# A gated attention and MLP decode step: small loads behind a first activation, and a last weight transfer in three pieces

## The chip, the cores and the metric

The kernel runs on one core of one Trainium2 chip. The metric is the device time of one execution in microseconds (us); lower is better. Three runs of the kernel before gave 137.19, 137.25 and 137.4 us, so the median is 137.25 us.

## What is computed

One token passes through two branches that a scalar gate mixes. The reference, cut to what matters:

```python
# x: 1 x 1 x 576 (A_x serves both branches); 32 query heads, 16 key/value heads, head size 128
W = 4096                                        # only the last 4096 positions of the cache are used
q = x @ wq                                      # 576 -> 32*128
k, v = k_cache[:, :, Sk-W:], v_cache[:, :, Sk-W:]   # 16 heads x 4096 x 128, bf16 each
a = softmax(q k^T * 128**-0.5) v @ wo           # 4096 -> 576
b = gelu(x @ w1 + b1) @ w2 + b2                 # 576 -> 4608 -> 576, tanh form of gelu
g = sigmoid((x * gate_w).sum())
out = g * a + (1 - g) * b
```

Nearly all of the bytes are read once: 16 heads of K and of V at 1 MB each, and four weight matrices of some 5 MB each, 53.6 MB in all. The arithmetic is small beside it.

## The kernel before

**Loads.** All big loads go out on SyncE's queue (SP). They come in this order: K of head 0 (line 89), two quarters of wq (line 106), K of head 1, the other two quarters of wq, then K and V tiles by turns with five pieces of w1 among them, then wo in four transfers (line 426), and at last w2 in four tiles `w2_t` of nine "rows" each (line 436; a row is 576 columns for each of 128 partitions). The first three w2 tiles come in one transfer each. The last one is cut in two by `cut = (0, 6, RJ)` on line 434: rows 0 to 5, then rows 6 to 8. The four small loads go out on ScalarE's queue (ACT): `x9` and `gw9` (line 117, x and the gate weights, 18 bytes for each of 128 partitions), `b1g` (line 118) and `b2_row` (line 119). They are the first instructions of ACT. The trace calls these loads x, gw, b1g and b_row, and w1 and w2 both w_t.

**What holds a load back.** K and V tiles share ten buffers, weights eight. Beyond that each load takes one of eight semaphores in turn, so that a ninth load is issued only when the one that had its semaphore has landed. In the trace of before, the first eight loads are the four small ones and K0, wq 0, wq 1 and K1. The third quarter of wq waits for x, the fourth for K0, K2 for gw, the first piece of w1 for b1g, K3 for b_row. All engines issue in the order in which the code is written (`manual_schedule`).

**Compute.** K tiles are transposed on TensorE (PE) against an identity matrix (line 189), four 128x128 blocks into one PSUM tile `tp`, of which there are three. VectorE (DVE, line 198) and ACT (line 200) copy these tiles to SBUF by turns. The scores (line 215), a softmax for each four heads (from line 233 on) and the values (line 275) follow, with lags of one to five heads. x is doubled into `x2` by four DVE instructions (line 179) that stand ahead of the first copy of line 198 in DVE's order. The gate is computed on lines 289 to 301, between the transposes of K0 and the product with wq (line 312). ACT's first instruction that needs a function table is the copy on line 200; `ident`, the identity, is built by GpSimd (POOL) from line 131 on.

**The end.** `row_matmul` (line 476) multiplies one row of wo or w2 in four matmuls of 144 columns, one for each quarter of the output. For w2, all rows of a tile follow each other, so the last tile takes 24 matmuls on rows 0 to 5 and 12 on rows 6 to 8. After the last one DVE forms `y` (line 506), and SP stores it (line 509).

Of the kernel before, what the change touches and what calls it, by code (L numbers as in the profile page):

```python
# [8 lines left out]
FP32 = mybir.dt.float32  # L9
BF16 = mybir.dt.bfloat16  # L10
ACT = mybir.ActivationFunctionType
# [5 lines left out]
def kernel(  # L17
# [15 lines left out]
    nc = tc.nc  # L33
# [11 lines left out]
    RJ = 9  # L45
    NG = F // (P * RJ)
# [22 lines left out]
    small = ctx.enter_context(tc.tile_pool(name="small", bufs=2))  # L69
# [42 lines left out]
    gw9 = const.tile([P, NM], BF16, name="gw9")  # L112
    b1g = const.tile([NG, F // NG], BF16, name="b1g")
    b2_row = const.tile([1, D], BF16, name="b2_row")
    for dst, src in ((x9, A_x.rearrange("a b d -> (a b d)")), (gw9, gate_w)):
        v = src.rearrange("(i o m) -> i o m", o=1, m=NM).to_broadcast([P // 2, 2, NM])
        nc.scalar.dma_start(out=dst[:], in_=v)
# [25 lines left out]
    for o in range(2):  # L143
        nc.vector.tensor_reduce(
            out=par[:, o : o + 1],
            in_=ident_f[:].rearrange("p (i o) -> p o i", o=2)[:, o, :],
# [7 lines left out]
        out=turn[:].rearrange("p j (h q) -> p j h q", h=OJ),  # L154
        in_=ident[:].rearrange("p (o q j) -> p j o q", o=1, j=OJ).to_broadcast(
            [P, OJ, OJ, P // OJ]
        ),
# [4 lines left out]
        out=m_r[:], in_=ident_f[:].rearrange("p (s r) -> p r s", r=R), axis=AX.X, op=ALU.add  # L162
# [3 lines left out]
        out=m_hl[:], in_=ident_f[:].rearrange("p (h q) -> p h q", h=OJ), axis=AX.X, op=ALU.add  # L166
# [117 lines left out]
    for i in range(NBL):  # L284
# [5 lines left out]
        out=junk9[:], in0=x9[:], in1=gw9[:], scale=1.0, scalar=0.0,  # L290
# [11 lines left out]
        out=omg[:], in0=g_t[:], scalar1=-1.0, scalar2=1.0, op0=ALU.mult, op1=ALU.add  # L302
# [20 lines left out]
    for g in (1, 3):  # L323
        for hl in range(HB):
            lo = R * g + 2 * hl
            nc.vector.tensor_copy(  # L326
                out=qz[:, hl::HB, lo : lo + 2],
                in_=q_ps[:].rearrange("p o (b r) -> p (o b) r", r=R)[:, :, 2 * hl : 2 * hl + 2],
# [95 lines left out]
    for i in range(NOG // 2):  # L424
        t = w_pool.tile([P, WMAX], BF16, name="wo_t", tag="w")
        nc.sync.dma_start(
            out=t[:, 0 : 2 * OJ * D].rearrange("p (o n) -> p o n", o=2),
            in_=wo_view[:, 2 * i : 2 * i + 2, :],
# [2 lines left out]
    w2_t = []  # L431
    for g in range(NG):
        t = w_pool.tile([P, WMAX], BF16, name="w2_t", tag="w")
        cut = (0, RJ) if g < NG - 1 else (0, 6, RJ)
        for lo, hi in zip(cut, cut[1:]):
            nc.sync.dma_start(out=t[:, lo * D : hi * D], in_=w2_view[g, :, lo * D : hi * D])
        w2_t.append(t)
# [4 lines left out]
        out=sg[:],  # L442
# [14 lines left out]
    for j in range(OJ):  # L457
# [3 lines left out]
        out=ow_m[:],  # L461
# [6 lines left out]
        out=ow_f[:].rearrange("p j o -> p (j o)"), in_=ow_m[:], axis=AX.X, op=ALU.add  # L468
# [17 lines left out]
    for o in range(NOG):  # L486
# [8 lines left out]
        out=a_sb[:], in0=a_ps[:], scalar1=g_t[:, 0:1], scalar2=None, op0=ALU.mult  # L495
# [5 lines left out]
    for g in range(NG):  # L501
# [5 lines left out]
        out=y[:], in0=b_ps[:], scalar=omg[:, 0:1], in1=a_sb[:], op0=ALU.mult, op1=ALU.add  # L507
    )
    nc.sync.dma_start(
        out=out.rearrange("a b (t n) -> (a b t) n", t=NQ), in_=y[0 : 32 * (NQ - 1) + 1 : 32, :]  # L510
# [31 lines left out]
```

## Time and profile before

| | |
|---|---|
| median of 3 runs | 137.25 us |
| the profiled execution | 137.34 us |
| its span (first to last instruction) | 135.5 us |
| mean granted TensorE clock | 0.779 |
| PE busy | 101.2 us, 75% |
| DVE busy | 57.4 us, 42% |
| ACT busy | 42.0 us, 31% |
| POOL busy | 1.4 us, 1% |
| moved by DMA | 53.88 MB, mean 398 GB/s over the span |
| chain that ended last | DMA 89%, PE 6% of the span |

The profiled execution takes 1.84 us more than its span; this rest lies outside the instructions. An engine's share of the span tells how long it worked, not whether anyone waited for it. The chain that ended last follows the waits back from the last instruction and is the better guide here. Of the DMA queues, q1 is SP's, q10 is ACT's, and q8 and q14 carry instructions ("instruction" in the page's third part). A DMA share of 1.00 means that all 16 DMA engines were busy.

### The profile page before, as it was taken

How to read it: one execution, taken by the hardware profiler on the slowest of the kernel's cores; microseconds unless marked ns; L12 is line 12 of the kernel's file. 1: busy time of each engine (PE TensorE's matmuls, PEld its weight loads, DVE VectorE, ACT ScalarE, POOL GpSimd, SP SyncE). 2: the span in 40 equal slices, each digit the busy share in tenths (PEclk: the TensorE clock that was granted, in tenths of full speed). 3: DMA queues.
4: the chain of work that ended last, by engine and by line, in shares of the span. 5: the costliest groups of instructions: out<-in, count | busy, mean ns of one | idle time of the engine just before them, and what ended most of it. 6: DMA issues, size and time to landing. Idle time of an engine off the chain costs nothing.

```text
span 135.5 us, 3928 instructions
## 1 busy us (share of the span) xinstructions
PE 101.2 (75%) x1779; PEld 81.8 (60%) x1779; DVE 57.4 (42%) x127; ACT 42.0 (31%) x75; POOL 1.4 (1%) x7
## 2 busy tenths in 40 slices
PE   0386857989969997979999986999695946343361
PEld 0376844668747876867868964788475844233350
DVE  5271521663468375735566357375732140010001
ACT  0360330454356165524356251554322000000000
POOL 4000000000000000000000000000000000000000
PEclk9999996589689999996589996589687555555555
DMA  4999999999999999999999999999999999999930
GB/s 116 412 428 419 418 432 430 424 421 428 426 423 428 430 412 426 423 431 419 432 424 423 426 415 429 426 418 426 428 423 426 420 416 424 424 434 419 401 126 3
DMA packets 8035, 53.88 MB, mean 398 GB/s; under 512 B 1101, under 2 KB 1102, under 8 KB 2514
## 3 DMA queue, kind: packets, MB, share of 16 engines
q1 hardware_dynamic: 7720, 53.61, 94.5%
q8 instruction: 14, 0.23, 0.6%
q10 hardware_dynamic: 298, 0.02, 0.1%
q14 instruction: 3, 0.02, 0.0%
HBM read 53.62 MB, written 0.00 MB: 396 GB/s over the span
## 4 chain that ended last, share of the span: by engine, by line
DMA 89%; PE 6%; DVE 1%; SPq 1%; issue 0%; DVEq 0%
DMA k_t<-in_A_k_cache_dram 30%; DMA w_t<-in_B_w_dram 15%; DMA wo_t<-in_A_wo_dram 15%; DMA v_t<-in_A_v_cache_dram 15%; DMA wq_t<-in_A_wq_dram 11%; DMA x<-in_A_x_dram 4%; PE tp L189 3%; PE s_ps L215 1%; PE o_ps L275 1%; DVE kT L198 1%; DVE mx L233 0%; PE b_ps L476 0%; PE mb L248 0%; SPq L96 0%; PE pT L260 0%
## 5 line engine op out<-in xcount | busy, mean ns | idle before, releaser
L189 PE MATMUL tp<-ident,k_t 128*128 128x128 bf16 x512 | 52.1, 252 | 10.6 <-DMA k_t<-in_A_k_cache_dram 8.6
L198 DVE CAST kT<-tp 128x512 bf16<-128x512 f32 x64 | 43.5, 690 | 33.8 <-PE tp L189 32.1
L200 ACT CAST kT<-tp 128x512 bf16<-128x512 f32 x64 | 37.5, 586 | 53.7 <-PE tp L189 53.3
L189 PEld LDWEIGHTS <-k_t 128*128 128x128 bf16 x512 | 37.4, 112 | 15.5 <-DMA k_t<-in_A_k_cache_dram 10.0
L275 PEld LDWEIGHTS <-v_t 128*128 128x128 bf16 x512 | 22.8, 103 | 6.6 <-issue 6.4
L275 PE MATMUL o_ps<-et,v_t 128*128 128x2 bf16 x512 | 26.3, 166 | 0.3 <-DVE et L264 0.3
L215 PE MATMUL s_ps<-kT,qz 128*32 128x512 bf16 x128 | 15.0, 465 | 0.7 <-DVE qz L326 0.7
L359 PE MATMUL h_ps<-x,w_t 128*128 128x2 bf16 x162 | 10.4, 199 | 0.0
L359 PEld LDWEIGHTS <-w_t 128*128 128x128 bf16 x162 | 10.1, 158 | 0.0
L476 PE MATMUL b_ps<-w_t,gt 128*1 128x144 bf16 x144 | 5.2, 319 | 5.7 <-DMA w_t<-in_B_w_dram 5.7
L476 PE MATMUL a_ps<-wo_t,ow 128*1 128x144 bf16 x128 | 4.5, 319 | 5.7 <-DMA wo_t<-in_A_wo_dram 4.5
L476 PEld LDWEIGHTS <-gt 128*1 128x1 bf16 x144 | 4.1, 115 | 6.7 <-issue 6.5
L476 PEld LDWEIGHTS <-ow 128*1 128x1 bf16 x128 | 3.6, 116 | 6.3 <-issue 5.2
L215 PEld LDWEIGHTS <-qz 128*32 128x32 bf16 x128 | 3.3, 95 | 4.5 <-issue 2.3
L312 PE MATMUL q_ps<-x,wq_t 128*128 128x2 bf16 x144 | 4.4, 166 | 2.0 <-DMA wq_t<-in_A_wq_dram 1.9
L312 PEld LDWEIGHTS <-wq_t 128*128 128x128 bf16 x144 | 4.2, 102 | 2.4 <-DMA wq_t<-in_A_wq_dram 2.4
L506 DVE SCALAR_TENSOR_TENSOR y<-b_ps,omg,a_sb 128x144 bf16<-128x144 f32 x1 | 0.4, 368 | 11.2 <-PE b_ps L476 11.2
L494 DVE TENSOR_SCALAR a_sb<-a_ps,g_t 128x144 f32<-128x144 f32 x1 | 0.4, 368 | 9.1 <-PE a_ps L476 9.1
L252 ACT ACTIVATE pr<-s_ps,nb 128x512 bf16<-128x512 f32 x4 | 2.7, 687 | 3.5 <-DVE nb L249 3.2
L237 PE MATMUL mT<-ident_f,mx 128*1 128x128 f32 x4 | 1.2, 295 | 3.4 <-DVE mx L233 3.4
L233 DVE TENSOR_REDUCE mx<-s_ps 128x1 f32<-128x512 f32 x4 | 2.7, 684 | 1.3 <-PE s_ps L215 1.3
L260 PE MATMUL pT<-ident,pr 128*128 128x128 bf16 x16 | 2.3, 289 | 0.7 <-ACT pr L252 0.7
(59 smaller groups left out, 26.3 us busy)
## 6 DMA issues: line engine op xcount, KB each, us to landing
k_t<-in_A_k_cache_dram SPq DMA_DIRECT2D x16, 1024.0 KB, 19.8
v_t<-in_A_v_cache_dram SPq DMA_DIRECT2D x16, 1024.0 KB, 19.7
wq_t<-in_A_wq_dram SPq DMA_DIRECT2D x4, 1152.0 KB, 12.1
w_t<-in_B_w_dram SPq DMA_DIRECT2D x4, 1152.0 KB, 20.5
wo_t<-in_A_wo_dram SPq DMA_DIRECT2D x4, 1152.0 KB, 21.0
w_t<-in_B_w_dram SPq DMA_DIRECT2D x3, 1296.0 KB, 21.4
w_t<-in_B_w_dram SPq DMA_DIRECT2D x1, 864.0 KB
w_t<-in_B_w_dram SPq DMA_DIRECT2D x1, 576.0 KB
```

The costliest lines, as they stand in the source:

```text
L189: nc.tensor.matmul(tp[:, c * P : (c + 1) * P], lhsT=k_tiles[h][:, i * BC + c, :], rhs=ident[:], start=True, stop=True,)
L198: nc.vector.tensor_copy(out=dst, in_=tp[:])
L200: nc.scalar.copy(out=dst, in_=tp[:])
L215: nc.tensor.matmul(s_tiles[b][32 * t : 32 * (t + 1), :], lhsT=qz[:, h, lo : lo + 32], rhs=kT[h][:, i * BC * P : (i + 1) * BC * P], start=( ...
L233: nc.vector.tensor_reduce(out=mx[:], in_=s_ps[:], axis=AX.X, op=ALU.max)
L237: nc.tensor.transpose(out=mT[:], in_=mx[:], identity=ident_f[:])
L252: nc.scalar.activation(out=pr[:], in_=s_ps[:], func=ACT.Exp, bias=nb[:, 0:1], scale=SCALE, accum_out=sums[:, b : b + 1],)
L260: nc.tensor.transpose(out=pT[:, c, :], in_=pr[:, c * P : (c + 1) * P], identity=ident[:])
L275: nc.tensor.matmul(o_ps[:, 2 * h : 2 * h + 2], lhsT=v_tiles[h][:, i * BC + c, :], rhs=ets[b][:, c, col : col + 2], start=(i == 0 and c == ...
L312: nc.tensor.matmul(q_ps[:, :, c], lhsT=wq_t[b // QP][:, off : off + Dh], rhs=x2[:, m, :], start=(b == 0), stop=(m == NM - 1), skip_group_c ...
L359: nc.tensor.matmul(h_ps[:, j, gl::GH], lhsT=t[:, off : off + U - RJ + 1 : RJ], rhs=x2[:, m, :], start=False, stop=(m == NM - 1), skip_grou ...
L476: nc.tensor.matmul(acc[32 * t : 32 * t + 1, :], lhsT=col, rhs=rows[:, t * DQ : (t + 1) * DQ], start=start, stop=stop,)
```

## The change

There are two edits.

1. Ahead of the small loads a one-element tile `warm` is set to zero by POOL and passed through `Exp` by ACT, in place. ACT issues in order, so its four small loads come behind this activation. The table load, which stood ahead of the first copy of line 200, comes ahead of the activation now. `warm` is read by nothing else.
2. The last w2 tile comes in three transfers, not two: rows 0 to 5, rows 6 and 7, and row 8. The matmuls and their order stay as they are.

```diff
     b2_row = const.tile([1, D], BF16, name="b2_row")
+
+
+    warm = small.tile([1, 1], FP32, name="warm", tag="warm")
+    nc.gpsimd.memset(warm[:], 0.0)
+    nc.scalar.activation(out=warm[:], in_=warm[:], func=ACT.Exp)
     for dst, src in ((x9, A_x.rearrange("a b d -> (a b d)")), (gw9, gate_w)):
         v = src.rearrange("(i o m) -> i o m", o=1, m=NM).to_broadcast([P // 2, 2, NM])
         nc.scalar.dma_start(out=dst[:], in_=v)
@@
         t = w_pool.tile([P, WMAX], BF16, name="w2_t", tag="w")
-        cut = (0, RJ) if g < NG - 1 else (0, 6, RJ)
+        cut = (0, RJ) if g < NG - 1 else (0, 6, 8, RJ)
         for lo, hi in zip(cut, cut[1:]):
             nc.sync.dma_start(out=t[:, lo * D : hi * D], in_=w2_view[g, :, lo * D : hi * D])
```

## The prediction

> **What bounds the kernel now.** I read the page's 40 slices first, then the chain that ended last, then the timeline of the last microseconds, and last the DMA share in short windows at both ends. All times are microseconds from the span's start.
>
> The page's DMA rows:
>
> ```profile
> DMA  4999999999999999999999999999999999999930
> GB/s 116 412 428 419 418 432 430 424 421 428 426 423 428 430 412 426 423 431 419 432 424 423 426 415 429 426 418 426 428 423 426 420 416 424 424 434 419 401 126 3
> ```
>
> From the second slice to the 38th the DMA engines are full. No engine's work counts there unless it empties SP's queue. What can move the time is the first slice, the last two, and the number of bytes or packets, and the change touches only these.
>
> The end, from the chain (start, length, what) and the timeline (start, length, engine, line, operation):
>
> ```profile
> 110.96 20.92 DMA w_t<-in_B_w_dram
> 131.88 0.04 issue
> 131.93 0.56 PE b_ps L476 x12
> ```
>
> ```profile
> 121.32 0.28 PE L476 MATMUL b_ps<-b_row,one_b 1*1 1x144 bf16 x4 [0.68 <-DVE b_ps L499]
> ...
> 130.88 0.89 PE L476 MATMUL b_ps<-w_t,gt 128*1 128x144 bf16 x24 [0.80 <-DMA w_t<-in_B_w_dram]
> ...
> 131.93 0.53 PE L476 MATMUL b_ps<-w_t,gt 128*1 128x144 bf16 x12 [0.16 <-DMA w_t<-in_B_w_dram]
> ...
> 132.51 0.37 DVE L506 SCALAR_TENSOR_TENSOR y<-b_ps,omg,a_sb 128x144 bf16<-128x144 f32 x1 [11.24 <-PE b_ps L476]
> 132.90 0.65 SPq L509 DMA_DIRECT2D out_dram<-y  x1
> ```
>
> The last three rows of w2 land at 131.88. Twelve matmuls (0.53), y and the store follow one after the other. Only the twelve matmuls can shrink here.
>
> The stream does not end at one moment. Windows of the end (stretch, length, busy time of PE, PEld, DVE, ACT, POOL, clock, DMA share, GB/s):
>
> ```profile
> 126.00:128.00 2.00, 0.96 (x34) 0.76 (x25) 0.00 (x0) 0.00 (x0) 0.00 (x0) 0.50 1.00 418
> 128.00:129.00 1.00, 0.17 (x8) 0.17 (x11) 0.00 (x0) 0.00 (x0) 0.00 (x0) 0.50 0.71 294
> 129.00:130.00 1.00, 1.00 (x36) 0.87 (x29) 0.00 (x0) 0.00 (x0) 0.00 (x0) 0.50 0.47 194
> 130.00:131.00 1.00, 0.20 (x12) 0.12 (x11) 0.00 (x0) 0.00 (x0) 0.00 (x0) 0.50 0.28 114
> 131.00:132.00 1.00, 0.84 (x28) 0.63 (x24) 0.00 (x0) 0.00 (x0) 0.00 (x0) 0.50 0.07 28
> ```
>
> A share of 0.28 is 4.5 of 16 engines. Some have finished by 129, and about five carry the end alone. A transfer lands with its slowest engine, so these few set the time. What made them late must be what not all engines carry alike. The page's instruction queue q8 is the candidate: 14 packets, 0.6% of 16 x 135.5, that is 13.0 in all and 0.93 for each, on one engine each.
>
> **Edit 2, the last tile in three transfers.** It removes nothing and adds one transfer. A piece has 128 partitions, so 8 packets for each of 16 engines, plus one that signals (q10's 298 packets are 261 rows of the four small loads and 37 more). So each engine gets 9 more packets. Their fixed price comes from the small loads, between 3 and 6:
>
> ```profile
> q10 hardware_dynamic: 168, 0.00, 3.1%
> ```
>
> 3.1% of 16 x 3 is 1.49, divided by 168: 9 ns, most of them 18 bytes. Nine of them are 0.08. The last landing goes from 131.88 to 131.96. Bounds: 0, and 0.25 if short packets cost three times as much.
>
> Behind it PE has 4 matmuls instead of 12. Four took 0.28 (b_row's row), 12 took 0.53, 24 took 0.89, so 8 more are about 0.25. Rows 6 and 7 land before row 8 by its 9 packets. Row 8 is a third of 432 KB, which took 131.88 - 130.84 = 1.04 in all (130.84 is the start at 130.88 less the same 0.04 of issue), so 0.35, and with its packets' price about 0.4. So their 8 matmuls (0.41 on that line) run from 131.6 to 132.0, just as row 8 comes. Then 131.96 + 0.05 + 0.28 = 132.29, against 132.46 now: **0.17 gained**. Bounds: 0.25 (free packets) and nothing (0.25 for packets). SP issues the extra load at about 113.7, when the second wo load returns its semaphore, 18 ahead of its landing. The store now waits for the third wo load's semaphore, back at 116.7 and long free at 132.5.
>
> The Trainium skill speaks against this edit: "DMA: Bandwidth & Descriptors", section Bandwidth (Measured), calls transfers under 64 KB descriptor-dominated and asks for 1 MiB or more, and its section on the anatomy of one DMA fits about 2.0 us fixed for each (on another issue path). The trace has a 432 KB transfer that lands 1.04 after the one ahead, about 425 GB/s, so that fixed part was hidden by the queue; by the page's fit unhidden, the sum would be near 139.
>
> **Edit 1, the loads behind an activation.** ACT's and SP's first rows:
>
> ```profile
> 0.73 0.62 ACTq L117 DMA_DIRECT2D x<-in_A_x_dram  x1
> 0.73 0.39 SPq L89 DMA_DIRECT2D k_t<-in_A_k_cache_dram  x1
> 1.19 0.90 SPq L106 DMA_DIRECT2D wq_t<-in_A_wq_dram  x2
> ...
> 2.13 0.78 SPq L89 DMA_DIRECT2D k_t<-in_A_k_cache_dram  x1
> ...
> 3.29 1.28 ACT L200 ACT_TABLE_LOAD   x1 [3.29 <-issue]
> ```
>
> *Moved on ACT.* The table load (1.28) goes to 0.73. The activation costs some 0.17 (ge, 128x1, line 296). So x is issued at about 2.2, 1.47 later, and gw, b1g and b_row as much. The four end at 4.8. The first copy on ACT starts at 6.62, so the table load was hidden and still is: **0**.
>
> *Who waits for x.* SP's third wq load waits for x's semaphore (2.8 by SP's waits) and goes out at 5.70; K2 (8.80) waits for gw, w1's first piece for b1g, K3 for b_row. Meanwhile K0, wq 0, wq 1 and K1 fill the queue until 13.91, when K1 lands. First packets come 1.03 after an issue (0.73 to about 1.76), so the third wq load may go out as late as 12.8: cover of 7.1 against 1.47. x landed 0.18 after K0, and gw 0.32 after wq 0 (8.47), so they may have waited for their turn behind these rather than for their issue. x lands between 5.7 and 7.2. Should the later place hand x a semaphore that follows SP's own loads, wq 2 waits for K0 (5.50) instead, the same.
>
> *Compute behind x.* DVE's four x2 instructions (5.78 to 6.41) stand ahead of its copies, so K0's transposes, the gate and the first wq products may come up to 1.5 later. PE then idles 1.30 until K1 lands and 1.69 until wq 3 (20.52): the lag is gone there. **0**. Without that cover it would be 1.5 on PE, but still not on the DMA stream, which PE reaches only through buffers.
>
> *POOL.* One memset more (0.1 by its rows) ahead of ident. DVE waits 2.53 for x behind that: **0**.
>
> *The stream's start.* Here is what may be won:
>
> ```profile
> 1.75:2.40 0.65, 0.00 (x0) 0.00 (x0) 0.62 (x7) 0.00 (x0) 0.23 (x1) 1.00 0.77 101
> 2.40:2.70 0.30, 0.00 (x0) 0.00 (x0) 0.30 (x3) 0.00 (x0) 0.00 (x0) 1.00 0.95 273
> 3.00:4.00 1.00, 0.00 (x0) 0.00 (x0) 0.25 (x2) 0.71 (x1) 0.00 (x0) 1.00 0.95 401
> ```
>
> In the first window 101 GB/s x 0.65 is 66 KB: eight packets of 8 KB. Half of the engines seem to start 0.65 late, and x's issue, 0.62 long, runs beside K0's. SP's first issues take 0.39, 0.45 (each of two) and 0.78, later ones 0.33. The bounds are 0 and 0.65 (where a late engine is also a last one). But the early eight packets were busy 0.77 x 16 x 0.65 = 8.0, 1.0 each, against 0.31 at full rate (8 KB at 428/16). So the early half had won almost nothing by 2.8, and the late half would win as little. I take 0.06 for K0's shorter issue (0.39 to 0.33) and 0.07 for the late half: **0.13 gained**.
>
> **Sum.** 0.17 + 0.13 = 0.30. The profiled execution goes from 137.34 (span 135.5, 1.84 around it) to 137.04 (span 135.2); the median, 0.09 below that execution, from 137.25 to **136.95**. A measurement of this kernel can tell some 0.2% (0.27) from no change; the forecast lies just beyond it.
>
> **Rivals.**
> - *Tail only.* The start has the same halves whether ACT issues or not, since the first packets' 1.0 sets it, and the packets of row 8 may eat more. 137.08 to 137.25. For it: those 1.0. Against it: the long SP issues. Chance 0.20.
> - *The late half comes in time.* All 16 engines start together and the last engines are of the late half: 0.35 (8 of 16 engines x 0.7) to 0.65 more than the tail alone, so 136.45 to 136.75. Against it: the 1.0 again. Chance 0.10.
> - *Slower: an instruction packet gets ahead of row 8.* One q8 packet starts at 132.04 now, just behind the stream; the window from 132 to 133 has its 16 KB. PE's progress seems to call it. With rows 6 and 7 started 0.3 earlier, it comes near 131.7. If it falls on one of the about five engines still streaming, before 131.96, row 8 lands some 0.93 later: 136.95 + 0.93 = 137.9. Five of 16 engines, less for timing: chance 0.12.
> - *The queue runs dry at the start.* It decides once x lands after about 12.8, as when ACT's loads wait for semaphores of big ones; each us beyond is one lost. Chance 0.06, 137.6 or more.
>
> **Chances.** The forecast has 0.52, about two thirds of it beyond 0.2%. Faster: 0.35 + 0.10 + 0.01 = 0.46. Same: 0.17 + 0.19 = 0.36. Slower: 0.18. The range 136.6 to 137.5 leaves out nearly all of the slower cases and the best start-up ones, 0.2 together.
>
> **What would show it.** ACT's table load stands at 0.73 and x's issue near 2.2. SP's first four issues shorten toward 0.33. If the start-up term is right, the first window has more than eight packets and K0 lands 0.1 before 5.50. If the covers hold, wq 3 is still what PE waits for near 20.4, and no DMA slice between is under 9. At the end, PE has a group of 8 and one of 4 matmuls, and y comes within 0.38 of the last landing (0.63 now). A last landing later than 131.96, or a third wq issue after 12.8, makes the prediction wrong.

## The result

The changed kernel takes 137.06 us (median of 22 runs, 136.7 to 137.53) against 137.36 us for the kernel before beside it (22 runs, 136.96 to 137.65). The ratio is 0.9981, with a 95% interval from 0.9973 to 0.9989: 0.26 us faster by the ratio (the two medians lie 0.30 apart), at the bound of 0.2% that was named. A second measurement gave 0.9987 (0.9973 to 1.0001). The forecast was 136.95 us, or 0.30 us faster.

**The profile after.** The DMA rows of the page have the same picture as before, a first slice not filled, then full, then two slices of end:

```profile
DMA  4999999999999999999999999999999999999930
GB/s 111 407 415 427 422 419 433 420 426 429 426 419 426 430 413 431 419 431 423 426 428 424 424 419 422 426 424 429 424 422 427 418 413 430 431 428 413 417 154 8
```

The first slice has not gained (111 GB/s, before 116). The timeline of the first microseconds shows why (start, length, engine, line, operation):

```profile
0.73 1.28 ACT L119 ACT_TABLE_LOAD   x1 [0.73 <-PEq L531]
0.73 0.09 POOL L118 MEMSET warm<- 1x1 f32 x1 [0.29 <-POOLq L531]
0.73 0.39 SPq L89 DMA_DIRECT2D k_t<-in_A_k_cache_dram  x1
...
0.86 0.64 ACTq L122 DMA_DIRECT2D x<-in_A_x_dram  x1
...
1.19 1.05 SPq L106 DMA_DIRECT2D wq_t<-in_A_wq_dram  x2
...
2.02 0.20 ACT L119 ACTIVATE warm<-warm 1x1 f32<-1x1 f32 x1
...
2.28 0.71 SPq L89 DMA_DIRECT2D k_t<-in_A_k_cache_dram  x1
...
5.66 1.46 PE L194 MATMUL tp<-ident,k_t 128*128 128x128 bf16 x12 [5.66 <-DMA k_t<-in_A_k_cache_dram]
```

x is issued at 0.86, while the table load is still running and 1.16 ahead of the activation. Here ACT's queue did not hold a DMA back for the engine's work in front of it. (The 0.13 fits the end of POOL's memset at 0.82, on which the activation itself waits; no run tests this.) So the small loads are behind the activation in the code only. They moved by 0.13 us (0.73 to 0.86) and not by 1.47, and SP's first four issues did not become shorter: 2.15 us in all (0.39, 1.05 and 0.71), before 2.07. K0 is there for PE at 5.66, 0.11 later than before:

```profile
5.55 3.88 PE L189 MATMUL tp<-ident,k_t 128*128 128x128 bf16 x32 [5.55 <-DMA k_t<-in_A_k_cache_dram]
```

The end, from the chain that ended last and from the timeline:

```profile
108.13 22.76 DMA w_t<-in_B_w_dram
130.89 0.04 issue
130.93 1.38 PE b_ps L481 x36
```

```profile
130.93 1.35 PE L481 MATMUL b_ps<-w_t,gt 128*1 128x144 bf16 x36 [0.81 <-DMA w_t<-in_B_w_dram]
...
132.34 0.37 DVE L511 SCALAR_TENSOR_TENSOR y<-b_ps,omg,a_sb 128x144 bf16<-128x144 f32 x1 [11.02 <-PE b_ps L481]
132.74 0.66 SPq L514 DMA_DIRECT2D out_dram<-y  x1
```

The chain is a different one now. Before, it ran from the landing of the last transfer at 131.88 to 12 matmuls. Now it runs from the landing of rows 0 to 5 at 130.89 to 36 matmuls without a gap: PE starts at 130.93 and is done at 132.31. By the trace's records of the semaphores, rows 6 and 7 landed at 131.64 and row 8 at 131.96, and PE did not wait for either. The wait of 0.16 ahead of the last twelve matmuls is gone, and so is the second start: 0.89 + 0.53 were 1.42, the 36 in one go are 1.35. y starts at 132.34, where the prediction had worked out 132.29 for the end of the matmuls, and 0.17 earlier than in the profile of before.

The last microseconds' windows (stretch, length, five engines' busy time, clock, DMA share, GB/s) show that the stream itself ends as before, with about five DMA engines of 16 (0.29 x 16 = 4.6) that carry it past 130:

```profile
129.00:130.00 1.00, 1.00 (x36) 0.91 (x29) 0.00 (x0) 0.00 (x0) 0.00 (x0) 0.50 0.53 212
130.00:131.00 1.00, 0.19 (x8) 0.07 (x7) 0.00 (x0) 0.00 (x0) 0.00 (x0) 0.50 0.29 115
131.00:132.00 1.00, 1.00 (x33) 0.81 (x32) 0.00 (x0) 0.00 (x0) 0.00 (x0) 0.50 0.12 44
```

### The profile page after: what moved, and what is told of

Read it like the earlier page. It is cut to its first block, busy times and chain, and to the rows that moved or that the text cites. A ratio compares the mean times of both kernels' runs of the same rounds, so it can differ in the third digit from the quotient of the medians.

```text
span 135.2 us, 3931 instructions
## 1 busy us (share of the span) xinstructions
PE 100.2 (74%) x1779; PEld 81.1 (60%) x1779; DVE 57.3 (42%) x127; ACT 42.1 (31%) x76; POOL 1.4 (1%) x8
## 3 DMA queue, kind: packets, MB, share of 16 engines
q1 hardware_dynamic: 7864, 53.61, 94.9%
## 4 chain that ended last, share of the span: by engine, by line
DMA 79%; PE 14%; DVE 3%; issue 1%; ACT 1%; ACTq 0%; SPq 0%; DVEq 0%
DMA w_t<-in_B_w_dram 31%; DMA k_t<-in_A_k_cache_dram 27%; DMA v_t<-in_A_v_cache_dram 15%; PE tp L194 6%; DMA b1g<-in_B_b_dram 6%; PE h_ps L364 3%; DVE kT L203 2%; PE s_ps L220 2%; PE b_ps L481 1%; ACT L119 1%; PE h_ps L352 0%; ACTq L122 0%; DVE mx L238 0%; PE o_ps L280 0%; DVE y L511 0%
## 5 line engine op out<-in xcount | busy, mean ns | idle before, releaser
L194 PE MATMUL tp<-ident,k_t 128*128 128x128 bf16 x512 | 51.3, 248 | 11.8 <-DMA k_t<-in_A_k_cache_dram 10.7
L194 PEld LDWEIGHTS <-k_t 128*128 128x128 bf16 x512 | 36.7, 111 | 16.7 <-DMA k_t<-in_A_k_cache_dram 12.2
L364 PEld LDWEIGHTS <-w_t 128*128 128x128 bf16 x162 | 10.1, 158 | 0.0
```

Of the source, the lines that this page charges most:

```text
L194: nc.tensor.matmul(tp[:, c * P : (c + 1) * P], lhsT=k_tiles[h][:, i * BC + c, :], rhs=ident[:], start=True, stop=True,)
L364: nc.tensor.matmul(h_ps[:, j, gl::GH], lhsT=t[:, off : off + U - RJ + 1 : RJ], rhs=x2[:, m, :], start=False, stop=(m == NM - 1), skip_grou ...
```

## The experiments

All ratios are against the kernel before on the same chip, with the 95% interval; the changed kernel has 0.9981. Differences in us are worked out from the ratios.

### Each edit alone

The first run keeps edit 1 only:

```diff
-        cut = (0, RJ) if g < NG - 1 else (0, 6, 8, RJ)
+        cut = (0, RJ) if g < NG - 1 else (0, 6, RJ)
```

> Edit 1 alone: the activation ahead of the small loads, the last tile still in two transfers. Theory (from the profile after): ACT's queue issues x at 0.86, while the table load is still running, so the loads move by 0.13 us only and the first packets start in the same two halves; the time is that of before, -0.05 to +0.1 us. Rival (the prediction's start-up term): SP's first issues become shorter and K0 lands earlier, 0.13 us faster than before.

Measured: 137.58 us, ratio 1.0005 (0.9997 to 1.0014). Edit 1 is worth nothing. x goes out at 0.86 here as well, K0 is there at 5.74.

The second run keeps edit 2 only, which is the kernel before with `cut = (0, 6, 8, RJ)`.

> Edit 2 alone: the last tile in three transfers, the loads as before. Theory: the whole gain is here. y starts 0.17 us earlier (132.34 against 132.51 in the profile of before), the end behind the store is 0.06 us shorter as in the profile after, so 0.2 to 0.3 us faster than before, as the two edits together. Rival: 0.17 us or less here, and the rest of the gain in edit 1.

Measured: 137.26 us, ratio 0.9977 (0.9962 to 0.9993), 0.32 us below before. The whole gain is in edit 2; the rival, a share for edit 1, falls with both runs.

The landing that ends the stream differs from execution to execution by more than the change moved it: 131.88 (before), 132.22 (edit 1 alone), 131.96 (changed), 132.37 (changed, second measurement), 132.13 (edit 2 alone). So a comparison of two profiles at that place says little, but two intervals inside each profile agree. From the landing of rows 0 to 5 to the last landing it is 1.046 in both kernels with two pieces, and 1.066 and 1.049 in these two with three (1.070 in the second measurement). From the last landing to the start of y it is 0.62 in both with two pieces and 0.39 in all with three. That is 0.24 gained on PE for 0.01 to 0.02 in the queue.

### The small loads made to wait

```diff
-    nc.scalar.activation(out=warm[:], in_=warm[:], func=ACT.Exp)
+    nc.scalar.activation(out=x9[0:1, 0:1], in_=warm[:], func=ACT.Exp)
```

> Both edits, but the activation writes its one element into x9, the tile that the load of x then overwrites, so that x must wait until the activation is done, as the prediction had thought that it would. Prediction: x is issued at 2.2 us, SP's first four issues go down toward 0.33 us each, more than eight packets start before 2.4 us, K0 lands 0.1 us earlier than 5.5; the time is 0.1 us below the changed kernel, and x's landing up to 1.5 us later costs nothing. Rival: the first eight packets start alone at 1.76 whoever issues beside them; same time as the changed kernel within 0.1 us.

Measured: 137.25 us, ratio 0.9988 (0.9976 to 0.9999), not to be told from the changed kernel; a gain of some 0.1 us more could hide in these intervals, so the start is read from the timeline:

```profile
0.73 0.39 SPq L89 DMA_DIRECT2D k_t<-in_A_k_cache_dram  x1
...
1.19 0.88 SPq L106 DMA_DIRECT2D wq_t<-in_A_wq_dram  x2
...
2.02 0.20 ACT L119 ACTIVATE x<-warm 1x1 bf16<-1x1 f32 x1
...
2.11 0.81 SPq L89 DMA_DIRECT2D k_t<-in_A_k_cache_dram  x1
...
2.26 0.61 ACTq L122 DMA_DIRECT2D x<-in_A_x_dram  x1
...
5.64 4.81 SPq L106 DMA_DIRECT2D wq_t<-in_A_wq_dram  x2
...
5.67 1.46 PE L194 MATMUL tp<-ident,k_t 128*128 128x128 bf16 x12 [5.67 <-DMA k_t<-in_A_k_cache_dram]
```

Here the loads stand where the prediction had put them, x at 2.26. Two things follow. The start shows no gain: SP's first four issues take 2.08 us without x beside them, and K0 is there at 5.67. And x's landing is far later than the 5.7 to 7.2 of the prediction: the issue of the last wq quarter waits for it until 10.1 (the two issues of that row last 4.81), so x took 7.8 us behind the big transfers. Nothing came of it at the end. The third wq quarter, which waits for K0 now, had been issued at 5.64 and landed at 16.8 only, so the queue had work for 6.7 us more when the fourth went out. The cover held.

The halves of the start differ from execution to execution, whoever issues. From 1.75 to 2.40 the windows give 101 GB/s in before and in the changed kernel, 202 with edit 2 alone (whose start is that of before) and 252 here:

```profile
1.75:2.40 0.65, 0.00 (x0) 0.00 (x0) 0.62 (x7) 0.46 (x2) 0.26 (x1) 1.00 0.92 101
```

```profile
1.75:2.40 0.65, 0.00 (x0) 0.00 (x0) 0.62 (x7) 0.46 (x2) 0.26 (x1) 1.00 0.78 252
```

The first of these is of the changed kernel, the second of this run. Twice the bytes and more, and K0 comes no sooner: 5.55, 5.66, 5.65 and 5.67 in the four.

### What a transfer more costs

All K tiles in two transfers each, `c` of 0 and NCH // 2:

```diff
+        for c in (0, NCH // 2):
+            nc.sync.dma_start(out=t[:, c : c + NCH // 2, :], in_=src[:, c : c + NCH // 2, :])
```

> Both edits, and every K tile also comes in two transfers of 4 KB a partition instead of one of 8 KB: 16 transfers more, so 16 x 9 = 144 packets more on each of the 16 DMA engines. Theory (9 ns for a packet's fixed price, as in the prediction): 144 x 9 ns = 1.3 us slower than the changed kernel, nothing else. Rival: the price is hidden, 0 to 0.3 us, and the 0.07 us by which the last landing came later after the change was chance. A price of 0.3 us or more for each transfer would give 5 us or more.

Measured: 138.57 us, ratio 1.0073 (1.0058 to 1.0088), 1.26 us above the changed kernel. That is the figure of the theory, but the landings told another story: the fourth wq quarter (20.57 in the changed kernel) landed at 21.44 already, so 0.9 of the loss seemed to lie in the start, which the theory does not explain. So a run with K0 and K1 whole was made:

> As the run with all K tiles in halves, but with K0 and K1 whole: 14 transfers more, all of them behind the start, where the stream is full. Reading of that run: of its 1.3 us, 0.9 was there by the time that wq 2 landed, and the rest is 0.03 us for each later transfer. By that, 0.4 us above the changed kernel. By the prediction's 9 ns for each of 9 packets, 14 x 0.08 = 1.1 us above.

Measured: 138.50 us, ratio 1.0067 (1.005 to 1.0085), 1.18 us above the changed kernel. The second reading, 0.03 for each transfer, was wrong, and the prediction's price stands. The 21.44 need not have been a loss at the start: in the kernels with whole K tiles the fourth wq quarter lands anywhere from 20.52 (before) to 21.42 (loads made to wait). The windows of the run with K0 and K1 whole, at the end, are those of the changed kernel one microsecond later:

```profile
129.00:130.00 1.00, 0.00 (x0) 0.00 (x0) 0.00 (x0) 0.00 (x0) 0.00 (x0) 0.50 0.88 349
130.00:131.00 1.00, 0.93 (x36) 0.93 (x36) 0.00 (x0) 0.00 (x0) 0.00 (x0) 0.50 0.51 202
131.00:132.00 1.00, 0.32 (x12) 0.11 (x2) 0.00 (x0) 0.00 (x0) 0.00 (x0) 0.50 0.32 124
```

0.51 and 0.32 are 0.53 and 0.29 of the changed kernel, shifted by one line. So all engines are late, not some, and 1.18 / 14 = 0.08 for each transfer of nine packets (with intervals of 0.1 and 0.2 us on the two times, 0.07 to 0.10). The trace has the price of the packets too: from 20 to 125 us a packet of 4 KB took 159 ns in the run with K0 and K1 whole, one of 8 KB 309 ns (medians), so two halves take 9 ns more than one whole. Packets of 4.6 and 9.2 KB, 178 and 347 ns in the changed kernel, give 9 ns as well. One more 8 KB packet of the second instruction queue (q14) that came into the stream at 95.8 took 0.31 us on one engine only.

The reverse was tried on wo, laid out with eight rows for each partition so that one run of 9.2 KB takes the place of two of 4.6 KB, 32 packets fewer on each engine:

```diff
-    OJ = 4
+    OJ = 8
```

> A version that uses the price of a packet: wo is laid out with eight rows for each partition instead of four (OJ = 8), so that its four transfers bring one run of 9.2 KB for each partition and not two of 4.6 KB. 32 packets fewer on each DMA engine; four more matmuls and a wider mask ahead of the wo products, 4 x 128 columns more in the turn matrix. Theory (9 ns a packet): 0.29 us below the changed kernel, near 136.8. Rival: the late engines are not bound by packets here, or the wider mask makes a_ps late: 0 or slower.

> The changed kernel itself beside the three others on the same chip: 0.998 of before within 0.001, as in the first measurement.

Measured side by side: 137.10 us, ratio 0.9981 (0.9969 to 0.9994), against 137.11 us, 0.9987 (0.9973 to 1.0001). The 0.29 us did not show in the time, though the two intervals, 0.17 us and more to either side, do not exclude it. It is not shown to be a version that beats the changed kernel. In the windows the early engines are done sooner (a share of 0.70 from 128 to 129, against 0.83 and 0.88 in the two profiles of the changed kernel), and the last ones are not clearly so (0.14 from 131 to 132, against 0.12 and 0.22). The landings agree: by the completion signals (explained below) the first engine is done with the last transfer at 128.35, against 128.70 and 128.69, which is about what 32 packets cost, and the last one at 132.03, against 131.96 and 132.37.

### Why some engines are late

The prediction had put down the late engines to instruction packets (q8). First these were to be made more, with tiny matmuls:

```diff
+        for _ in range(4):
+            nc.tensor.matmul(tp[0:1, 0:1], lhsT=one_b[:], rhs=one_b[:], start=True, stop=True,
+                             skip_group_check=True)
```

> The changed kernel with four more pairs of weight load and matmul (one by one element, into a place of tp that the transposes then overwrite) ahead of each of the 128 tiles of transposes: 512 pairs, 1024 instructions more on PE. An instruction packet of 16 KB comes about every 256 instructions of PE (3571 instructions, 14 packets), so 18 packets instead of 14. Theory: these packets go round a part of the DMA engines (13 before the end of the stream, about five late engines), so the four more fill up the others and one engine gets its third; it ends about 1 us later and the time is 0.7 to 1.2 us above the changed kernel. Rival A: each packet costs the stream 0.93/16 us, so 0.25 us for four. Rival B: the late engines have nothing to do with instruction packets: 0, unless PE itself becomes late, which the DMA slices would show as less than full.

> The same with two pairs for each tile: 256 pairs, 512 instructions, two packets more. Theory: these two fall on engines that had one such packet, so none ends later than the latest now: within 0.15 us of the changed kernel, with one or two more late engines in the last microsecond but one. Rival A: 0.12 us. Rival C (every packet delays the latest engine): 1 us or more, as far as two packets go.

Measured: 169.73 us, ratio 1.2337 (1.2315 to 1.236), and 165.06 us, ratio 1.2011 (1.1989 to 1.2033). Both say nothing on the question, since PE had become the bound. The page of the second one shows it by a chain of 78% PE and a DMA row that is no longer full:

```profile
DMA  5999999999999992999770799690936999999500
```

Then the packets were made fewer. Left out: most of the values and of the product with w1, and three eighths of the scores, so that PE has 1368 instructions less. All loads are as in the changed kernel.

```diff
-        for c in range(BC):
+        if i == 0:                                   # values: one matmul a head
...
-            for j in range(RJ):
+            for j in range(RJ if u >= 16 else int(u == lo)):      # w1: 22 of 162
...
-            if i in (2, 5) and h < Hkv:
+            if (i == 2 or (i == 5 and h % HB == HB - 1)) and h < Hkv:
```

> The changed kernel with work on PE left out, so that its instructions fit into fewer packets; every load is as before. Left out: of the values all but one matmul for each head, of the product with w1 all but 22 of 162 matmuls, and the second half of the scores in three of four heads. That takes 1368 of 3571 instructions from PE, and leaves 8 instruction packets instead of 14 ahead of the end. Theory: the late DMA engines are those with two packets; with one at most on each, the last landing comes 0.7 to 1.2 us earlier (near 131.0) and the time is 0.5 to 0.9% below the changed kernel. Rival: the late engines are late for another reason, and the last landing stays near 132.

Measured: 135.9 us, ratio 0.9876 (0.9859 to 0.9893), 1.4 us below the changed kernel and more than was expected. Its page and its windows:

```profile
q8 instruction: 8, 0.13, 0.3%
```

```profile
129.00:130.00 1.00, 0.62 (x24) 0.62 (x24) 0.00 (x0) 0.00 (x0) 0.00 (x0) 0.50 0.51 190
130.00:131.00 1.00, 0.72 (x24) 0.35 (x12) 0.23 (x1) 0.00 (x0) 0.00 (x0) 0.50 0.01 2
```

Up to 130 the stream runs down as in the changed kernel (0.51 against 0.53). Then there is nothing: the last landing is at 130.39. The five engines that carried the end for 1.6 us more are not there. The time alone does not tell fewer instructions from less work on PE, but the traces do. Each big transfer is recorded with 16 completion signals, read here as one from each DMA engine. Behind the first of the 16, the others come as follows:

| kernel, landing of | q8 packets so far | engines within 1.2 us | one step late | two steps late |
|---|---|---|---|---|
| changed, K1 (14.16) | 0 | 16, all within 0.6 | none | none |
| changed, third wq quarter (17.84) | 1 | 15 | 1, at 1.5 | none |
| changed, a K or V tile (87.26) | 8 | 8 | 8, at 1.4 to 1.8 | none |
| changed, a K or V tile (90.83) | 9 | 8 | 7, at 1.5 to 1.8 | 1, at 2.9 |
| changed, row 8 (131.96) | 13 | 8 | 3, at 1.6 | 5, at 2.8 to 3.3 |
| less PE work, row 8 (130.39) | 8 | 8 | 8, at 1.4 to 1.8 | none |

Each packet makes one more engine late, and it stays late to the end. The first eight fall on eight different engines, the ninth (at 88.62) on one that had its packet already, and 13 make five engines with two and three with one: 5 x 2 + 3. With eight packets no engine has two. The first signal of row 8 comes at the same time in both kernels (128.70 and 128.64), so the early engines did not gain by the lighter PE work. (Of the eight that are not late two are 0.7 to 1.2 behind; they fell back when the two 8 KB packets of q14 came into the stream.) A second packet sets its engine back by some 1.2 to 1.7 us, more than the 0.93 that it takes itself, which would explain why the gain was more than expected. So the end of this kernel is set by the DMA engines that bring instructions for PE, as the prediction supposed. Which engine a packet ran on is not in the trace; that it is the one that becomes late is read from the times and the counts.

### The end behind the store

In the profile after, the time from the store's issue to the end of the span is 2.51 us, before it was 2.57. At the end SP waits for the eight semaphores in a fixed order, and one transfer more hands the store the semaphore that is last in it. Two single runs move the store's semaphore by splitting the first w2 tile too; the edit of the first of them:

```diff
+        cut = {0: (0, 5, RJ), NG - 1: (0, 6, RJ)}.get(g, (0, RJ))
```

> The kernel before with the first w2 tile in two transfers, the last one still in two: one transfer more ahead of the store, as in the changed kernel, but 12 matmuls behind the last landing. Theory: y starts 0.62 us after the last landing, as before; the time from the store's issue to the end of the span goes from 2.57 to 2.51 us, since the store now signals the semaphore that SP waits for last at the end. Rival: that time is 2.57 and belongs to the cut of the last tile or to chance.

> The changed kernel with the first w2 tile in two transfers as well: two transfers more than before ahead of the store, so its semaphore is the next in turn, one of those that SP waits for early at the end. Theory: y starts 0.38 us after the last landing; from the store's issue to the end 2.6 us or more, since further waits follow the store's. Rival: 2.51 us as in the changed kernel.

Measured: 2.51 and 2.59 us, and y 0.62 and 0.38 behind the last landing. In all profiles of the runs above, it is 2.49 to 2.52 where the store has the last semaphore, and 2.56 to 2.61 in the four where it has another (before, edit 1 alone, K0 and K1 whole, and the second of these two). So some 0.06 us of the gain goes with the place in this order. (The times, 137.63 and 137.6 beside 137.41 for before, are of one execution each, and nothing is read from them.)

## Why the prediction was right, and where it was not

**The total** was 0.30 and is 0.26 (by the first measurement), and the direction and the part that carries it are right. Its two terms are not. The tail was put at 0.17 and the start at 0.13. The runs give 0.22 to 0.23 for the tail, 0.06 for the end behind the store, and nothing for the start (1.0005 with edit 1 alone). That the total came so close is luck: gains that were not seen made up for one that is not there.

**The step of edit 1 that failed** is "so x is issued at about 2.2, 1.47 later". It took ACT's order for granted, table load, activation, loads, one after the other. The trace has x go out at 0.86, during the table load. Even where they do wait, the start gains nothing. The 0.07 for the late half was too much and the 0.06 for K0's issue too: K0's issue stays at 0.39 beside nothing at all (with the loads at 2.26). The argument in the same paragraph, that the first packets' 1.0 us sets the start, was the better one, and the rival "Tail only" had it. (By its own rows the four small issues would have ended at 4.7, not 4.8; nothing rests on it.)

**The covers of edit 1** held: the table load, POOL's memset, and x's landing. The bound for x's landing did not: 5.7 to 7.2 was said, 10.1 came once x was issued at 2.26. The queue never ran dry. That the semaphores might be handed out in another order was right: the third wq quarter waits for K0 now (5.63), the fourth for x.

**Edit 2.** "So their 8 matmuls (0.41 on that line) run from 131.6 to 132.0, just as row 8 comes" was wrong in its start: PE works on rows 0 to 5 until 131.8 (in the prediction's own line until 131.77), and the eight follow without a gap. The groups of 8 and of 4 that were to show it are one group of 36. The end comes out the same, since both limits, row 8's landing with four matmuls behind it (132.29) and PE's chain from 130.93 (132.31), now lie within 0.05 us of each other. The nine packets on each engine are right: q1 has 7864 packets against 7720 before, and 144 is 16 x 9. Their price, 0.08, is right for a full stream (0.08 in the run with 14 more transfers) and too high at the very end, where 0.01 to 0.02 was seen; why it is less there stays open. The 0.4 for row 8 was too much too: it landed 0.32 behind rows 6 and 7. A last landing later than 131.96 was named as a sign of being wrong, but it is none: that landing varies from execution to execution by more than the change moves it (131.96 and 132.37 in the two profiles of the changed kernel).

**The rule on small transfers** that was weighed against edit 2 had no say here: 144 KB behind 288 KB came 0.32 us after it (131.96 - 131.64), so no fixed cost of its own is to be seen.

**The slower rival**, an instruction packet ahead of row 8, did not happen at its place: the packet came at 132.12 in the profile after, behind the last landing. But its cause is real: an engine that gets such a packet is late from then on, and with eight packets instead of 14 the stream ended 1.6 us earlier.

## What to carry to other kernels

Behind a stream that a queue keeps full, the gain is in what follows the last landing: cut the last transfer so that the work on each piece is just done when the next one lands, and stop there, since the next limit is PE's own chain. Before a load is moved "behind" an instruction of the same engine, see in the trace whether the queue issues it early; here only a wait held it back. And look at the end of a DMA-bound kernel engine by engine: some 423 GB/s in the full slices hid that five of 16 engines ended 2.8 to 3.3 us behind the first, each with two packets of PE's instructions. There, fewer PE instructions can shorten the DMA stream, though PE itself has time to spare.

## What was new about the hardware

- ACT's queue issued a DMA at 0.86, beside a table load that ran from 0.73 to 2.01, and ahead of an activation at 2.02. With a wait on the activation's result it was issued at 2.26.
- A small load issued behind big transfers took 7.8 us to land, where the same load beside the first transfer took 4.9.
- The activation started 0.01 after the table load's end. The Trainium skill, "ScalarE: Activation LUTs", section What ACT_TABLE_LOAD costs, gives 1283 ns, which the trace shows to the nanosecond, and a drain of 1380 ns beside it for every switch to a different set, of which this first load shows nothing.
- Instruction packets of PE (16 KB, 14 of them for 3571 instructions) use the same DMA engines as the loads, eight of them in turn by the completion signals, and here they decide which engine ends last: an engine with one such packet ended 1.6 us behind the first, one with two 2.8 to 3.3. The Trainium skill, "Runtime: NRT & Kernel Launch", section Instruction fetch mechanics, describes these blocks and calls the cost of crossing one mostly hidden; in this kernel, which is bound by DMA, the run with six packets fewer (and much less PE work) was 1.4 us faster.
- Tiny matmuls are not free among large ones: 256 pairs on one element took PE's busy time from 100.2 to 145.2 us and the time from 137.1 to 165.1 us, the next 256 by only 4.7 more. Both runs have them at the same 128 places, and the transposes behind them went from 51.3 us busy to 77.9 and 77.7: the cost goes with the places more than with the pairs. Why stays open.
